# GpSimd leaves the experts' weights: ScalarE makes every hi part, VectorE every lo part

## The chip, the cores and the metric

One core of a Trainium2 chip runs the whole program. The metric is device time in microseconds; "before" is the median of three runs. The profile is one execution of the same program, and its times count from the first instruction.

## The reference

The program chains an attention with pooled queries, a layer of eight experts with top-1 routing, and a dense layer with a cosine gate. What matters here is the middle:

```python
x = attention output, 2304 tokens x 512
do_compute = (x @ w_skip) > 0
logits = xc @ w_gate;  e_idx = argmax(logits)          # eight experts
for e in range(E):
    h = np.maximum(xc[mask] @ w1[e], 0.0)              # 512 x 1024
    y[mask] = gate_w[mask, None] * (h @ w2[e])         # 1024 x 512
out[do_compute] = xc + y
```

All is float32. The kernel keeps that precision by splitting every operand of a product into a rounded hi part and the rest, the lo part, and adding three products (hi by hi, lo by hi, hi by lo).

## The kernel before

**Stages.** Attention runs until about 559 us of the profile, the experts from there to about 762 us, the last layer to the end. Only the experts' stage contains what is changed.

**Pieces of weights.** An expert's weights are eight pieces of 128 x 1024 float32 (512 KB): four of w1, four of w2. Eight experts give 64 pieces, numbered in `self.count` in the order in which `Experts.piece` is called. For each piece, SyncE's queue issues a load into one of six staging buffers (L699; the first six are loaded before the stage begins), one engine copies it to the hi part (L706 GpSimd or L708 ScalarE, a rounding copy), and one engine subtracts to make the lo part (L709, GpSimd or VectorE). hi and lo lie in `whl`, which has ten buffers: piece k + 10 can be made only when TensorE has done with piece k. A staging buffer is free for the next load when both parts are made.

**Which engine makes which part** stands in two lists by hand: 18 of the 64 hi parts (`HPOOL`) and 15 of the lo parts (`LPOOL`) are GpSimd's. A loop at the end that takes left-over blocks has lists of its own (`HREST`, `LREST`); for these inputs it runs no round, as the counts of 64 hi and 64 lo parts in the trace show.

**Blocks.** An expert's tokens go in blocks of 256, 128 or 64 rows; `GROUPS` says which expert by rank has which blocks, thirteen in all. Four experts have a single block of 64 rows, so a whole expert's weights are made for little TensorE work. A block is transposed (`transposed`, TensorE to PSUM, then ScalarE L686 makes hi and VectorE L687 lo), multiplied with w1 (`mm1`), its hidden rows are made (L746/L747 for 256 rows; L754, L755 and the transposes with L683/L684 for 64 rows), multiplied with w2 (`mm2`), and scaled by the gate (L798, L800). Tokens are fetched and results scattered by indirect transfers that GpSimd issues (L633, L801).

**Routing of the last batch** lies at the start of the stage: GpSimd adds the last logits (L336 to L343), VectorE runs a chain of small operations (L469 to L511), a small product of TensorE stands in that chain (L497 to L502), and GpSimd scatters the lists (L519). The second weights of the first expert (pieces 4 to 7) are asked for with `issue_after(self.placed.ins)`: what they issue on VectorE stands behind the end of that chain (L511); what they issue on other engines does not.

**Order.** A planner turns the program into one fixed queue per engine before the run: it goes through the program by priority, which is mostly program order, with its own idea of durations, and gives an engine the first instruction that it holds to be ready. On the chip every engine takes its queue in order, and waits at the head of it.

Of the kernel before, what the change touches and what calls it, by code (L numbers as in the profile page):

```python
# [8 lines left out]
F32 = mybir.dt.float32  # L9
# [9 lines left out]
NB, NH, NS, ND = 4, 8, 1152, 64     # batches, heads, keys, head width  # L19
NQ = NS // 2                        # pooled queries of a batch  # L20
NT = NB * NQ                        # tokens
DM, NE, FF, FF2 = 512, 8, 1024, 2048
CAP = NT                            # list rows an expert has: every token fits
NJ = 12                             # entries of the tables of pairs and of single blocks
LIST = NE * CAP + 128 * 28          # the rest of the list stays empty
TR = 4 * NJ + 1                      # where the ranks of experts start in the tables
BIG = 1 << 20                       # a row index that is out of bounds everywhere
# The blocks of rows that experts take: the one with the most tokens of all batches but the last, a first block of
# FIRST rows and then these; the others by their rank in how many tokens they have. A loop takes all that is left
# [4 lines left out]
NXT = 6                             # buffers for gathered tokens  # L34
QS = -0.0625                         # halves the sum of two queries, and scales scores by -1 / sqrt(ND)
OFFS = {'s0': 3, 's1': 2, 'r0': 2, 'r1': 2, 'n': 2, 'e0': 2, 'e1': 2, 't0': 1, 't1': 1, 's2': 2, 'r2': 2, 'e2': 1, 'h1': 1}
POOLP = ((5, 1), (6, 2), (7, 0))  # (chunk, piece) whose p parts GpSimd makes
STEPS = 'l1 r0 h0 e2 p4 s1 t2 s2 r2 l0 r1 h2 n x t1 t0 l2 e1 f s0 e0 p3 p2 a h1 p4'
NCH = 6
POPS = (0, 7, 8)               # chunks after which a step of the routing goes  # L40
# [6 lines left out]
LAG = 5                             # products that the second ones of the last layer run behind  # L47
ORDERS = ('1 1 1 1 r 1 w t g g g h', '2 2 2 2 2 x x g 1 1 1 1 1 h', '1 2 1 2 1 2 x 2 1 1 g 2 h', '1 x 1 1 1 g 2 2 2 1 h 2 2', '1 1 2 x 1 1 2 1 h 2 2 g 2', '1 1 1 2 x 2 1 2 2 1 h 2', 'x 1 g 1 1 1 2 1 h 2 2 2 2', '1 g 1 1 1 1 x 2 2 2 2 2 g h', '1 1 x 1 1 1 h 2 2 2 2 2', 'g 1 1 1 x 2 1 2 2 1 h 2 2 g', '1 1 x 1 1 2 2 1 2 h 2 2', '1 1 1 x 2 2 1 2 2 1 h 2', '1 1 1 2 1 2 1 2 h 2 2')
ORDER = "1 1 x 1 1 1 2 2 h 2 2 2 g"    # steps of a block that is left
HPOOL = (5, 7, 8, 15, 21, 29, 36, 37, 39, 42, 45, 47, 48, 52, 53, 54, 58, 62)  # L50
LPOOL = (6, 9, 11, 16, 21, 22, 23, 30, 38, 40, 45, 56, 57, 62, 63)
HREST, LREST = (1, 4, 6), (3,)


class Attention:
    def __init__(self, tc, ctx, stage, q, k, v, ident, pair_done, extra=lambda: None, last=lambda c: None, n_pairs=16):
# [5 lines left out]
        # the first to be free at the end come first, where the experts' first weights go  # L62
# [14 lines left out]
        # sums of the parts of a chunk's rows, and what is added to them  # L77
# [16 lines left out]
    def start(self):  # L94
        """load the first pair and make its operands: each head's q and k go to both halves of the partitions"""
        nc, s = self.nc, self.st.setdefault(0, {})
        raw = self.pb.tile([128, 9, 640], F32R, name="ptbigh").bitcast(F32).rearrange("p a b -> p (a b)")
        # the first activation loads its table, which need not wait for data
# [54 lines left out]
    def preps(self, i):  # L153
        """the steps that make pair i's operands, in order"""
# [55 lines left out]
    # chunk order within a pair, with the column it takes in its pT tile  # L210
# [4 lines left out]
    def scores(self, i, c, n):  # L215
        """a third of the scores of a chunk, times -1 / sqrt(ND)"""
        nc, s = self.nc, self.st[i]
        kind, j = self.CH[c]
        if kind == "X":
            qx, khl = s["qx"], s["khl"]  # L220
            prods = [(qx[:, 0, :], khl[:, 0, :]), (qx[:, 1, :], khl[:, 0, :]), (qx[:, 0, :], khl[:, 1, :])]
        else:
            h = 0 if kind == "A" else 1
            qa, k1 = s["qa"][h], s["k1"][h]
            prods = [(qa[:, t, 128 * j:128 * j + 128], k1) for t in range(2)]
        o = s["s", c, n] = self.pss.tile([128, 512], F32, name="s")
        for t, (w, m) in enumerate(prods):
            nc.tensor.matmul(o[:, 0:384], w, m[:, 384 * n:384 * n + 384], start=t == 0, stop=t == len(prods) - 1)  # L228
# [53 lines left out]
    # AV groups: head, pT tile, first column, columns, chunks whose sums they need  # L282
# [3 lines left out]
    def av_ops(self, i, key):  # L286
        """the steps of an AV group, in order, as callables"""
# [32 lines left out]
    def out_part(self, i, key):  # L320
        """token-major output of an AV group, and what it adds to the routing logits"""
# [5 lines left out]
        # the third has only 64 rows; what stands in the others goes nowhere  # L327
# [79 lines left out]
class Router:  # L407
    """top-1 routing: per expert a list in DRAM of (token, gate) pairs, in regions of CAP rows"""
# [9 lines left out]
    def start(self):  # L418
# [6 lines left out]
        # constants: e * CAP, 8 - e, valid rows, token numbers, counting matrices  # L425
# [14 lines left out]
        # tri[k, m] = 1 where k < m  # L440
# [11 lines left out]
        # per head: what sums the two halves of an output of attention, and gives its logits  # L452
# [6 lines left out]
    def route(self, b, L, ps, tag="tp"):  # L459
        """the lists' entries of a batch from its logits; a list of steps"""  # L460
# [4 lines left out]
    def choose(self, b, L, box):  # L465
# [15 lines left out]
        # the first expert that has the maximum  # L481
# [10 lines left out]
    def place(self, ps, tag, box):  # L492
        """place within the expert: tokens before it in its tile, in earlier tiles, in earlier batches"""
# [24 lines left out]
    def scatter(self, t, box):  # L518
# [3 lines left out]
        # the rows that different scatters write are different  # L522
# [4 lines left out]
    def counts(self, ps, tag):  # L527
        """how many tokens each expert has so far, and numbers in that order that are all different"""
# [6 lines left out]
    def ahead(self, ps, tag, tab):  # L535
        """the expert with the most tokens so far, whose first block is taken as it is now: in tab from TR + 2 NE on, its
        number, the first list row of its region, and the first one that is left"""
# [15 lines left out]
    def rank(self, ps, tag, tab):  # L553
        """the experts in the order of how many tokens they have, but the one whose first block has been taken as the
        last: in tab from TR on, their numbers, then the first list rows of their regions. In begin, the tokens of each
        that the blocks of its rank take"""
# [23 lines left out]
    def plan(self, ps, tag, tab):  # L580
        """the blocks of the other tokens, as pairs and at most one single block per expert. In tab, NJ
        each: experts and first list rows of the pairs, then those of the single blocks; last, the loop's end"""
# [11 lines left out]
        # blocks, pairs, single ones of each expert, and of one more that has no tokens and no end  # L594
# [33 lines left out]
def gathered(nc, pool, xg, lt, name, xt=None, n=NT, rows=128):  # L628
    """the tokens of a list; rows that no token fills keep what was there, and are dropped in the end"""
# [8 lines left out]
class Experts:  # L638
    def __init__(self, tc, ctx, stage, early, xts, w1, w2, ident, xg, x2, lst):
# [4 lines left out]
        # a pool has to wait for all that lay where it lies: the first weights have one of their own  # L644
# [19 lines left out]
    def transposed(self, srcs, nch, rows, relu=False):  # L664
        """hi and lo parts of the transposes of the column blocks of one or two sources of 128 rows, or of one of 64:
        then, lo stands beside hi"""
# [23 lines left out]
    def piece(self, w, e, c, n):  # L690
# [9 lines left out]
        hp, lp = (self.count in HPOOL, self.count in LPOOL) if self.laid_out else (n in HREST, n in LREST)  # L700
# [4 lines left out]
        if hp:  # L705
            nc.gpsimd.tensor_scalar(hi, raw, 1.0, 0.0, ALU.mult, ALU.add)  # L706
        else:
            nc.scalar.copy(hi, raw)  # L708
        (nc.gpsimd if lp else nc.vector).tensor_tensor(lo, raw, hi.bitcast(F32), ALU.subtract)  # L709
        return hi, lo  # L710

    def weights(self, group, k, c):
        """pieces up to c of an expert's first (k = 0) or second weights, which all its blocks use"""
        w = group["w"][k]
        while len(w) <= c:
            w.append(self.piece((self.w1, self.w2)[k], group["e"], len(w), 4 * k + len(w)))
        return w[c]

    def mm1(self, group, xT, rows):
        """steps: four products, and what leads to the hidden rows (one block) or their transposes (two)"""  # L720
# [4 lines left out]
        def product(c):  # L725
            hi, lo = self.weights(group, 0, c)
            if rows == 256:
                # the weights stay put, and both blocks pass them
# [36 lines left out]
    def products(self, o, xT, rows, c, hi, lo, first, last, b=0):  # L765
        """adds the products of a block's rows with a piece of weights: of 64 rows, hi and lo parts pass hi as one, and
        what they give is still to be added"""
# [13 lines left out]
    def mm2(self, group, hT, g, rows):  # L781
        """steps: four products, and the rows of the result"""
# [26 lines left out]
    def run(self, groups, first=None, route=None, plan=None):  # L809
        """groups: functions that give an expert and the first list row of its blocks, and the blocks' rows with where  # L810
        they start; first: the lists of the first block, if it is there before the others, which route (a list of
        steps) and plan then make"""
        self.laid_out = first is not None
# [61 lines left out]
def narrow(nc, pool, src, tag, g=None, n=512):  # L875
    """n columns of float64, which come as pairs of int32 words, as float32"""
# [5 lines left out]
    # sign and top exponent bit, the low 7 exponent bits, 23 bits of the mantissa  # L882
# [3 lines left out]
    # what is below float32's range (an exponent under 897, read as a float32 one: 2^-15) becomes zero  # L886
# [7 lines left out]
class Ffn:  # L894
    """out = (h cos h) w_out, h = x w_in"""
# [42 lines left out]
    def xT(self, x, tags):  # L938
        """hi and lo parts of a chunk's transpose, and the steps that make them"""
# [14 lines left out]
    def hidden(self, x, f, m):  # L954
        """what leads to hi and lo parts of -g / 2 = (sin^2(r / 2) - 1 / 2) h, r = h - 2 pi k: r, and a step for the
        rest"""
# [37 lines left out]
    def run(self):  # L994
# [3 lines left out]
        # two chunks of 384 tokens at a time  # L998
# [85 lines left out]
def build(tc, q, k, v, wg, ws, w1, w2, w_in64, w_out64, out):  # L1084
    nc = tc.nc
    w_in64, w_out64 = w_in64.bitcast(I32), w_out64.bitcast(I32)
    with ExitStack() as top:
# [9 lines left out]
        with ExitStack() as mid:  # L1097
# [9 lines left out]
            # staging buffers that attention loads into, and then the experts, whose first weights come before its end  # L1107
# [6 lines left out]
            def ranked(j):  # L1114
                """the expert of rank j: its number, its first list row"""
# [97 lines left out]
```

## Time and profile before

| | |
|---|---|
| runs | 1210.28, 1212.82, 1219.66 us; median 1212.82 |
| profiled execution | span 1214.5 us, the only time given of it |
| experts' stage in it | about 559 to 762 us |
| TensorE's mean granted clock | 0.978 of 2.4 GHz |
| hi parts of pieces | 46 by ScalarE, 18 by GpSimd |
| lo parts of pieces | 49 by VectorE, 15 by GpSimd |

In the rows below PE is TensorE's products, PEld its weight loads, DVE is VectorE, ACT ScalarE, POOL GpSimd. A line number is that of the kernel before. An arrow in brackets names what ended a wait.

### The profile page before, as it was taken

Reading aid. Unit: us, or ns where it says so; the run is one execution under the profiler, and the core shown is the slowest. Engines: PE = TensorE matmul, PEld = TensorE weight load, DVE = VectorE, ACT = ScalarE, POOL = GpSimd, SP = SyncE. Lnnn points to the kernel's source line nnn. Section 1 sums busy time; section 2 is a strip of 40 time slices with the busy share of each in tenths; the row PEclk is TensorE's granted clock in tenths of the full one; section 3 lists DMA queues with packets and bytes.
Section 4 is the critical chain, followed back from the end, with each engine's and each line's share of the span. In section 5 each row is a group of like instructions: output and inputs, shape, how many; then the busy total and the mean of one; then the engine's idle time right before and its main releaser. Section 6 shows DMA issues by size and latency. Waiting matters only on the chain. (4 is left out here: it accounts for less than half of the span.)

```text
span 1214.5 us, 20655 instructions
## 1 busy us (share of the span) xinstructions
PE 1124.1 (93%) x6722; PEld 1006.4 (83%) x6722; DVE 952.4 (78%) x1942; ACT 758.1 (62%) x1998; POOL 650.0 (54%) x861
## 2 busy tenths in 40 slices
PE   3999999999999999997989997688997999999998
PEld 3989899899898999897767874578886999889987
DVE  7889899999899999897788667498898755565554
ACT  3889898899888999795245312444544544454343
POOL 7587667766577666736656525265454423222331
PEclk9999999999999999998999998889999999999999
DMA  6575566456765675433568534632221200010001
GB/s 180 141 200 146 152 202 177 125 154 166 215 168 141 162 212 142 115 101 122 176 217 290 174 99 148 195 97 79 55 68 35 105 1 1 1 53 1 1 1 53
DMA packets 62639, 147.73 MB, mean 122 GB/s; under 512 B 17882, under 2 KB 17882, under 8 KB 62528
## 3 DMA queue, kind: packets, MB, share of 16 engines
q1 hardware_dynamic: 59840, 141.75, 40.4%
q0 software_dynamic: 2688, 4.62, 1.1%
q8 instruction: 55, 0.90, 0.3%
q14 instruction: 56, 0.46, 0.1%
HBM read 91.93 MB, written 21.69 MB: 94 GB/s over the span
## 5 line engine op out<-in xcount | busy, mean ns | idle before, releaser
L237 DVE TENSOR_REDUCE m<-s 128x1 f32<-128x384 f32 x432 | 236.7, 552 | 49.0 <-PE s L228 38.4
L246 ACT ACTIVATE p<-s,m 128x384 f32<-128x384 f32 x432 | 247.8, 583 | 22.4 <-DVE m L241 19.5
L228 PE MATMUL s<-k,qa 128*128 128x384 f32 x768 | 228.9, 382 | 32.1 <-ACT p L246 16.9
L264 PE MATMUL tp<-ident,p 128*128 128x128 f32 x1296 | 203.8, 277 | 4.6 <-DVE ptsml L280 2.3
L264 PEld LDWEIGHTS tp<-ident,p 128*128 128x128 f32 x1296 | 164.1, 143 | 17.8 <-issue 2.2
L228 PEld LDWEIGHTS s<-k,qa 128*128 128x128 f32 x768 | 120.4, 195 | 41.6 <-ACT p L246 26.0
L966 ACT ACTIVATE t<-hp,magic 128x384 f32<-128x384 f32 x96 | 55.6, 579 | 138.6 <-PE hp L963 137.1
L963 PE MATMUL hp<-fxh,wih 128*128 128x384 f32 x384 | 131.7, 344 | 8.5 <-ACT h L967 7.2
L968 POOL TENSOR_SCALAR t<-t 128x384 f32<-128x384 f32 x96 | 60.5, 631 | 135.5 <-ACT t L966 132.6
L963 PE MATMUL hp<-fxl,wih 128*128 128x384 f32 x384 | 130.3, 339 | 0.0
L963 PE MATMUL hp<-fxh,wil 128*128 128x384 f32 x384 | 130.2, 339 | 0.0
L992 PE MATMUL o<-woh,gh 128*128 128x512 f32 x288 | 115.7, 402 | 3.2 <-ACT woh L926 3.2
L992 PE MATMUL o<-wol,gh 128*128 128x512 f32 x288 | 115.5, 401 | 1.5 <-DVE wol L929 1.5
L992 PE MATMUL o<-woh,gl 128*128 128x512 f32 x288 | 115.0, 399 | 0.0
L280 DVE TENSOR_TENSOR ptbigl<-tp,ptbigh 128x384 fp32r<-128x384 f32 x208 | 112.3, 544 | 0.1
L978 POOL TENSOR_SCALAR gh<-h 128x384 fp32r<-128x384 f32 x96 | 70.4, 746 | 77.6 <-DVE h L976 69.2
L969 DVE TENSOR_TENSOR r<-t,h 128x384 f32<-128x384 f32 x96 | 67.4, 702 | 52.1 <-POOL t L968 51.6
L976 DVE SCALAR_TENSOR_TENSOR h<-r,h 128x384 f32<-128x384 f32 x96 | 56.4, 622 | 57.7 <-ACT r L975 57.7
L275 ACT CAST ptbigh<-tp 128x384 fp32r<-128x384 f32 x208 | 94.0, 490 | 11.2 <-PE tp L264 10.5
L280 DVE TENSOR_TENSOR ptsml<-tp,ptsmh 128x384 fp32r<-128x384 f32 x176 | 95.1, 545 | 0.7 <-ACT ptsmh L275 0.7
L275 ACT CAST ptsmh<-tp 128x384 fp32r<-128x384 f32 x176 | 81.4, 489 | 21.0 <-PE tp L264 15.4
L709 DVE TENSOR_TENSOR whl<-stage,whl 128x1024 fp32r<-128x1024 f32 x49 | 79.5, 1644 | 16.6 <-POOL whl L706 11.6
(239 smaller groups left out, 2906.2 us busy)
## 6 DMA issues: line engine op xcount, KB each, us to landing
stage<-w SPq DMA_DIRECT2D x64, 512.0 KB, 4.1
k<-stage SPq DMA_DIRECT2D x60, 288.0 KB, 5.4
qa<-stage SPq DMA_DIRECT2D x60, 256.0 KB, 5.1
stage<-v SPq DMA_DIRECT2D x16, 576.0 KB, 6.4
stage<-q SPq DMA_DIRECT2D x15, 576.0 KB, 4.7
stage<-k SPq DMA_DIRECT2D x15, 576.0 KB
wiw<-w_in SPq DMA_DIRECT2D x16, 512.0 KB, 4.5
wow<-w_out SPq DMA_DIRECT2D x16, 512.0 KB, 3.7
```

What stands on the lines that cost most here:

```text
L228: nc.tensor.matmul(o[:, 0:384], w, m[:, 384 * n:384 * n + 384], start=t == 0, stop=t == len(prods) - 1)
L237: self.last_max = nc.vector.tensor_reduce(s["m", c][:, n:n + 1], s["s", c, n][:, 0:384], AX.X, ALU.min)
L246: self.nc.scalar.activation(s["p", c][:, 384 * n:384 * n + 384], s["s", c, n][:, 0:384], AF.Exp, bias=s["m", c][:, 3:4], scale=-1.0, accum ...
L264: nc.tensor.transpose(tp[:, a, :], p[:, (3 * n + a) * 128:(3 * n + a + 1) * 128], self.ident)
L275: self.nc.scalar.copy(hi, tp)
L280: self.nc.vector.tensor_tensor(lo, tp, hi.bitcast(F32), ALU.subtract)
L709: (nc.gpsimd if lp else nc.vector).tensor_tensor(lo, raw, hi.bitcast(F32), ALU.subtract)
L963: nc.tensor.matmul(hp, w[:, d], a[:, d], start=d + k == 0, stop=d == 3 and k == 2)
L968: nc.gpsimd.tensor_scalar(t, t, -self.MAGIC, -self.C1, ALU.add, ALU.mult)
L969: nc.vector.tensor_tensor(r, t, h, ALU.add)
L978: nc.gpsimd.tensor_scalar(gh, h, 1.0, 0.0, ALU.mult, ALU.add)
L992: self.nc.tensor.matmul(o[t], a[:, s], w, start=f + k == 0, stop=f == 15 and k == 2)
```

## The change

In `piece` the choice of engine is gone: the hi part is always ScalarE's copy and the lo part always VectorE's subtraction. The lists `HPOOL`, `LPOOL`, `HREST`, `LREST`, the flag `laid_out` and the argument `n` that only fed them go with it. The rest of the diff removes comments.

```diff
-HPOOL = (5, 7, 8, 15, 21, 29, 36, 37, 39, 42, 45, 47, 48, 52, 53, 54, 58, 62)
-LPOOL = (6, 9, 11, 16, 21, 22, 23, 30, 38, 40, 45, 56, 57, 62, 63)
-HREST, LREST = (1, 4, 6), (3,)
...
-    def piece(self, w, e, c, n):
+    def piece(self, w, e, c):
...
-        hp, lp = (self.count in HPOOL, self.count in LPOOL) if self.laid_out else (n in HREST, n in LREST)
...
-        if hp:
-            nc.gpsimd.tensor_scalar(hi, raw, 1.0, 0.0, ALU.mult, ALU.add)
-        else:
-            nc.scalar.copy(hi, raw)
-        (nc.gpsimd if lp else nc.vector).tensor_tensor(lo, raw, hi.bitcast(F32), ALU.subtract)
+        nc.scalar.copy(hi, raw)
+        nc.vector.tensor_tensor(lo, raw, hi.bitcast(F32), ALU.subtract)
...
-            w.append(self.piece((self.w1, self.w2)[k], group["e"], len(w), 4 * k + len(w)))
+            w.append(self.piece((self.w1, self.w2)[k], group["e"], len(w)))
```

## Rows read from the trace of the kernel before

**Rows 1.** The page's first part: busy us, share of the span, instructions.
```profile
PE 1124.1 (93%) x6722; PEld 1006.4 (83%) x6722; DVE 952.4 (78%) x1942; ACT 758.1 (62%) x1998; POOL 650.0 (54%) x861
```

**Rows 2.** Busy time by stretch: us, each engine, granted clock, DMA share, GB/s.
```profile
555.00:762.00 207.00, 183.00 (x968) 142.33 (x966) 152.98 (x216) 70.17 (x96) 113.29 (x78) 0.95 0.52 179
...
560.00:580.00 20.00, 14.38 (x99) 13.74 (x100) 11.36 (x26) 3.51 (x7) 14.68 (x17) 0.83 0.44 147
...
600.00:680.00 80.00, 74.88 (x403) 57.01 (x403) 69.06 (x71) 38.97 (x51) 53.69 (x30) 0.98 0.72 252
...
620.00:640.00 20.00, 15.90 (x69) 11.11 (x67) 17.31 (x16) 8.70 (x10) 14.87 (x9) 0.91 0.72 234
...
680.00:700.00 20.00, 16.98 (x104) 14.98 (x103) 11.20 (x11) 4.15 (x6) 6.64 (x4) 0.91 0.37 124
...
740.00:760.00 20.00, 13.92 (x57) 8.32 (x56) 16.87 (x17) 4.40 (x6) 14.13 (x7) 0.88 0.33 107
```

**Rows 3.** TensorE's waits, 550 to 765 us: total us, times, longest.
```profile
PE ops L773 <- DVE hTh L684: 6.3, 3, 3.1
PE tp L680 <- DVE hs L755: 4.9, 5, 2.4
PE hps L734 <- DVE hTl L747: 3.0, 1, 3.0
PE rk L497 <- DVE oh L489: 2.4, 1, 2.4
...
PE ops L779 <- DVE whl L709: 0.3, 1, 0.3
```

**Rows 4.** Timeline of PE where the last layer begins.
```profile
768.87 0.90 PE L948 MATMUL o<-ident,fx 128*128 128x128 f32 x3 [7.97 <-DMA fx<-x]
```

**Rows 5.** Groups by line, 550 to 760 us: busy us, mean ns, idle before.
```profile
L709 DVE TENSOR_TENSOR whl<-stage,whl 128x1024 fp32r<-128x1024 f32 x49 | 79.5, 1644 | 16.6 <-POOL whl L706 11.6 <-ACT whl L708 5.0
L708 ACT CAST whl<-stage 128x1024 fp32r<-128x1024 f32 x46 | 47.6, 1052 | 40.8 <-DMA stage<-w 22.3 <-PE hps L773 9.9 <-issue 2.7
...
L709 POOL TENSOR_TENSOR whl<-stage,whl 128x1024 fp32r<-128x1024 f32 x15 | 40.4, 2702 | 9.6 <-ACT whl L708 9.3
...
L706 POOL TENSOR_SCALAR whl<-stage 128x1024 fp32r<-128x1024 f32 x18 | 20.6, 1153 | 25.2 <-PE hps L773 18.7 <-DMA stage<-w 6.3
```

**Rows 6.** The line of the lo parts: duration ns min/median/max, first and last start.
```profile
L709 DVE TENSOR_TENSOR whl<-stage,whl x49: 1206/1224/3427, 555.6 to 753.6; 128x1024 fp32r<-128x1024 f32 x49
```

**Rows 7.** Timeline of the stage's start, POOL, DVE and PE: start, us.
```profile
560.32 2.02 POOL L706 TENSOR_SCALAR whl<-stage 128x1024 fp32r<-128x1024 f32 x1
...
565.05 2.37 POOL L709 TENSOR_TENSOR whl<-stage,whl 128x1024 fp32r<-128x1024 f32 x1 [1.87 <-ACT whl L708]
...
565.11 2.34 DVE L477 TENSOR_SCALAR gate<-gate 128x5 f32<-128x5 f32 x1
...
565.02 0.38 PE L734 MATMUL hps<-xTl,whl 128*128 128x256 f32 x1 [1.65 <-DVE xTl L687]
```

**Rows 8.** Timeline around 622 us, POOL, DVE and PE.
```profile
620.73 2.41 POOL L709 TENSOR_TENSOR whl<-stage,whl 128x1024 fp32r<-128x1024 f32 x1
...
620.80 3.42 DVE L709 TENSOR_TENSOR whl<-stage,whl 128x1024 fp32r<-128x1024 f32 x1 [1.25 <-POOL whl L706]
...
625.54 0.80 PE L773 MATMUL ops<-whl,hTh 128*128 128x512 f32 x1 [3.06 <-DVE hTh L684]
```

**Rows 9.** Timeline around 683 us, DVE, POOL and PE.
```profile
679.70 4.82 DVE L709 TENSOR_TENSOR whl<-stage,whl 128x1024 fp32r<-128x1024 f32 x2
...
680.18 3.26 POOL L709 TENSOR_TENSOR whl<-stage,whl 128x1024 fp32r<-128x1024 f32 x1
...
686.62 0.54 PE L734 MATMUL hps<-xTh,whl 128*128 128x256 f32 x2 [3.02 <-DVE hTl L747]
```

**Rows 10.** Groups by line, 600 to 680 us.
```profile
L709 DVE TENSOR_TENSOR whl<-stage,whl 128x1024 fp32r<-128x1024 f32 x26 | 42.2, 1640 | 6.2 <-POOL whl L706 3.2 <-ACT whl L708 3.0
...
L709 POOL TENSOR_TENSOR whl<-stage,whl 128x1024 fp32r<-128x1024 f32 x9 | 22.9, 2548 | 4.5 <-ACT whl L708 4.4
```

More of the change, by code (lines that the diff above doesn't have):

```diff
@@ L809, in run @@
     def run(self, groups, first=None, route=None, plan=None):
-        self.laid_out = first is not None
         groups = [{"get": get, "base": base, "blocks": blocks, "w": ([], [])} for get, base, blocks in groups]
```

## The prediction

> **What bounds the kernel now.** I read the page's first part, then busy time by stretch, then what TensorE waits for. TensorE is busy 93% of the span [rows 1], so the question is only what it loses in the stage that is changed. That stage lasts 207 us, and no engine but TensorE is near full: 183.0 us TensorE, 153.0 VectorE, 113.3 GpSimd, 70.2 ScalarE; DMA is at 0.52 [rows 2]. TensorE hardly ever waits for a piece itself: 0.3 us once. It waits for VectorE's other work: the lo part of a 64-row block's hidden rows (6.3 us), its two halves' sum (4.9), the hidden rows of a 256-row block (3.0), the routing (2.4) [rows 3]. These operations stand behind lo parts of pieces in VectorE's queue. Each such wait is seen again in the granted clock: it is 0.83 in 560 to 580 us and 0.91, 0.91 and 0.88 in the stretches of the later waits [rows 2]. With levels of 1 and 0.5, that is TensorE work lost of 20 x 0.17 = 3.4 us, then 1.8, 1.8 and 2.4. At the stage's end TensorE waits 7.97 us for the last layer's tokens [rows 4]; nothing of the change lies there.
>
> So at most some 25 to 30 us of the stage can be won: waits of about 17 us [rows 3] and 9.4 us of clock.
>
> **Part 1: what each part costs on its engine.** A lo part takes VectorE 1.22 us at the median, but 1.644 at the mean and 3.43 at most [rows 5, 6]. The long ones lie where GpSimd runs a part of its own: at 620.80 VectorE's took 3.42 us, and GpSimd's had begun at 620.73 and taken 2.41; VectorE's ended 1.1 us after it, as if it had begun when GpSimd's ended [rows 8]. At 679.70 two took 4.82 us around one of GpSimd's [rows 9]. A small step of the routing chain, on 128 x 5 numbers, took 2.34 us from 565.11; GpSimd's lo part ran from 565.05 for 2.37 [rows 7]. So a part on GpSimd holds up VectorE, and what the lists were to save is largely paid back.
>
> The sum for VectorE: 15 lo parts more at 1.22 = +18.3 us. Relief: 49 x (1.644 - 1.224) = -20.6 us [rows 5, 6], and 2.2 us of the routing step. VectorE ends at 153.0 + 18.3 - 22.8 = 148.5 us: no more than before. In the dense stretch, 600 to 680 us, it is 9 x 1.22 = +11.0 against 26 x 0.416 = -10.8 [rows 10]. Bounds of the relief: all of it, or none if the length has another cause; I take all, since the three rows above fit to 0.2 us.
>
> ScalarE gets 18 hi parts at 1.05 = +18.9 us, and has 70.2 of 207 [rows 2, 5]: throughput covers it. GpSimd loses 40.4 + 20.6 = 61 us [rows 5]; it is then left with indirect transfers, which come no later. Loads: a staging buffer is free when both parts are made, 1.05 + 1.22 = 2.3 us of work on ScalarE and VectorE in place of 1.15 + 2.70 = 3.9 where GpSimd made both [rows 5], so SyncE's queue is not held longer on that account; DMA at 0.72 in the dense stretch has room [rows 2].
>
> **Part 2: what lies on the path,** from the profile's span of 1214.5 us, which is 1.7 above the median of the runs.
>
> *Start, 560 to 570 us.* GpSimd's lo part no longer stands before the routing step, which ends about 2.2 us sooner. On VectorE this piece goes behind the chain, by the order that the code writes for pieces 4 to 7. The 2.4 us wait for the routing falls by 2.2. GpSimd's hi part of 560.32 (2.02 us) stands before its last logits, on which the chain hangs, and the 1.65 us wait before may shrink with it [rows 7]. Against it, that hi part now can stand before the first tokens' hi part on ScalarE: 0 to 1.05. I take -2.2 + 0.5 = -1.7 (bounds -4.0 to +1.1). Of the clock's 3.4, half: -1.7 (0 to -3.4), since a shorter wait may still lower it.
>
> *622 us.* The lo part in the way falls from 3.42 to 1.22, and GpSimd's part of 620.73 becomes one more of 1.22 that may stand there too: -1.0 (-3.1 to +0.3) of a wait of 3.06. Clock: a third of 1.8, -0.6.
>
> *683 us.* Two lo parts fall from 4.82 to 2.44, one comes: -1.2 (-3.0 to 0) of 3.02. Clock -0.6.
>
> *740 to 760 us.* Four lo parts come to VectorE, 4.9 us, in the last 64-row blocks, against relief of about the same size; 0 (-2.5 to +2.5), and of 2.4 us of clock nothing.
>
> *ScalarE's queue.* GpSimd's hi parts stood waiting 25.2 us, 18.7 of it for TensorE to release a buffer and 6.3 for a load [rows 5]. These waits now stand at the head of ScalarE's queue, with evacuations of PSUM (L686, L683, L746) behind them, and TensorE and VectorE wait for those. Bounds: 0, if the planner puts them where ScalarE is idle anyway, to +8, a third. As ScalarE is idle two thirds of the time, +1.0.
>
> Sum: -1.7 - 1.7 - 1.0 - 0.6 - 1.2 - 0.6 + 0 + 1.0 = **-5.8 us**: 1208.7 by the profile, **1207** by the median of the runs.
>
> The Trainium skill, "Perfetto Trace Analysis", section "Optimizing Scalar/DVE Operations", says that where VectorE is saturated, giving work to ScalarE or even GpSimd may make sense, which speaks against this change, and in the same paragraph that GpSimd and VectorE share a read port, so that moving work between those two might not help. By the first sentence alone the lists are worth the 18.3 us that they spare VectorE, and the outcome is the rival "VectorE becomes the bound"; by the second it is the sum above. The rows of 620.80 and 565.11 bear out the second; no row shows VectorE full over a stretch.
>
> **The rivals.**
> *All of it comes back.* If each of the first three waits falls below what lowers the clock, waits and clock go together: -4.0 - 3.4 - 3.1 - 1.8 - 3.0 - 1.8 = -17, and with +1 for ScalarE -16: 1197. For: clock and waits lie together in every stretch of rows 2. Against: in two of the three places an added lo part may stand in the same spot.
> *VectorE becomes the bound (slower).* If the long lo parts don't shorten as said, the stretch from 600 to 680 us has 69.06 + 11.0 = 80.1 us of VectorE work in 80 [rows 2, 10]; its queue never empties, every evacuation in it comes later, and TensorE pays the 11.0, less some 3 won at the start: +8, 1221; with all 18.3 unpaid, 1231. It decides from the point where less than about half of the 10.8 comes back. Against: three rows that fit.
> *ScalarE's queue holds.* A hi part that waits for a buffer or a load stands before an evacuation several times: +8 in place of +1, which gives 1214, and with the first places won only by half 1217. For: ScalarE's own hi parts already wait 22.3 us for loads and 9.9 for buffers [rows 5]. Against: the planner hands out what it holds ready.
> *Nothing to be seen.* Relief and addition fall on the same places and the planner's new order wins as much as it loses: 1213.
>
> **How the numbers follow.** Forecast (1202 to 1212) 0.47, all back 0.17, VectorE the bound 0.13, ScalarE's queue 0.11, nothing 0.12. The range leaves out the better half of "all back" and the upper half of "VectorE": 1197 to 1225. One per cent, 12 us, is about what a measurement here can tell from no change (the three runs span 0.8%). Below 1200.7: "all back" and a little of the forecast's edge, 0.18. Above 1225: most of "VectorE" and an edge of "ScalarE's queue", 0.12. Within: 0.70.
>
> **What would show it.** Right: all 64 lo parts on VectorE near 1.22 us, mean under 1.3; VectorE's busy time in the stage at or under 153; the routing step short, and TensorE's wait for the routing under 1 us; shorter waits for L684 and L747; a clock above 0.83 in the first stretch. Wrong: lo parts still long without GpSimd; a stretch in which VectorE has no idle time; ScalarE's hi parts waiting with L683, L686 or L746 late behind them; or the planner's new order moving TensorE's work in a way that no step here names.

## The result and the profile after

The changed kernel takes 1199.57 us (median of four runs, 1194.12 to 1202.32) against 1211.63 of the kernel before on the same chip (median of four). The ratio on record is 0.9865, with a 95% interval of 0.9831 to 0.9899; it is not the ratio of these two medians, which is 0.990. By it the change is worth 16 us; the medians lie 12.1 us apart, and the spans of the two profiled executions 13.9. 5.8 were forecast. All us given for runs below are worked out from the ratio on record and the median of the kernel before. The profiled execution has a span of 1200.6 us; its run is listed with 1202.32, so 1.7 us lie around the span.

The page's first part, which answers to [rows 1]. GpSimd loses 66 us, ScalarE gains 18, and VectorE, which has 15 more lo parts to make, is busy 6 us less.
```profile
PE 1119.4 (93%) x6722; PEld 1002.4 (83%) x6722; DVE 946.3 (79%) x1957; ACT 775.9 (65%) x2016; POOL 584.4 (49%) x828
```

Busy time by stretch (us; each engine; granted clock; DMA share; GB/s): first the stage, then its start and the stretches that answer to those around 620, 683 and 750 us of [rows 2].
```profile
554.00:747.00 193.00, 180.68 (x971) 140.80 (x969) 146.75 (x232) 88.42 (x115) 48.47 (x46) 0.96 0.55 192
559.00:579.00 20.00, 17.75 (x121) 16.79 (x121) 12.21 (x34) 7.49 (x12) 10.56 (x14) 0.83 0.44 151
617.00:637.00 20.00, 19.94 (x95) 14.05 (x95) 19.20 (x22) 11.69 (x14) 6.64 (x4) 1.00 0.80 275
672.00:692.00 20.00, 19.90 (x138) 17.59 (x138) 10.88 (x14) 6.49 (x10) 1.89 (x2) 1.00 0.46 161
725.00:745.00 20.00, 14.35 (x57) 9.17 (x56) 15.75 (x19) 5.47 (x7) 3.29 (x2) 0.83 0.31 101
```
TensorE's products fill the second and third of these short stretches (19.9 of 20 us, clock 1.00, where before they had 15.9 and 17.0 at 0.91). The last stretch is no better than before.

The line of the lo parts (min/median/max ns), which answers to [rows 6]:
```profile
L702 DVE TENSOR_TENSOR whl<-stage,whl x64: 1206/1215/1483, 555.0 to 740.5; 128x1024 fp32r<-128x1024 f32 x64
```
The groups of both parts in the stage, which answer to [rows 5]:
```profile
L702 DVE TENSOR_TENSOR whl<-stage,whl 128x1024 fp32r<-128x1024 f32 x64 | 76.6, 1221 | 11.1 <-ACT whl L701 10.9
L701 ACT CAST whl<-stage 128x1024 fp32r<-128x1024 f32 x64 | 66.2, 1054 | 55.5 <-DMA stage<-w 39.8 <-PE hps L772 5.8 <-SPq L1175 4.9
```
TensorE's waits in the stage, which answer to [rows 3]; the wait for the last layer's tokens is left out:
```profile
PE ops L766 <- DVE hTh L681: 2.2, 1, 2.2
PE tp L677 <- DVE hs L748: 2.0, 2, 1.5
PE hps L766 <- DVE xTh L684: 1.8, 1, 1.8
PE hps L765 <- DVE whl L702: 1.5, 1, 1.5
```
Without GpSimd's parts no lo part takes longer than 1.48 us, where the longest was 3.43. Sixty-four of them cost VectorE 76.6 us, less than the 49 before. The waits for the 64-row hidden rows and the halves' sums fell from 11.2 to 4.2 us; those for the routing and for the 256-row hidden rows are gone. The one for the first tokens of the second expert has grown from 0.33 to 1.8, and one for a lo part is new (1.5). VectorE's own waits for hi parts fell from 16.6 us [rows 5] to 10.9.

**Where the time went.** Both kernels do the same products, so TensorE's progress can be laid side by side: us from the stage's first transposition until so many thousand columns had passed TensorE, worked out from the start times of all its products (a transposition of 64 columns and less counted as 64). Each column is one profiled execution of a run named in the experiments below; after_again is the changed kernel a second time.
```
columns  before   after  after_again  read_dummies  write_dummies  lo_only  hi_only  tail_lo
   20k     17.73   14.40        11.78         12.68          11.79    14.41    11.79    14.11
   40k     26.88   23.54        20.93         22.35          20.94    23.57    20.96    23.28
   60k     36.89   34.99        32.91         36.67          32.32    33.60    38.62    34.71
  100k     57.65   55.73        53.65         57.40          53.06    54.35    59.32    55.45
  140k     83.76   76.29        74.26         78.75          73.59    75.24    79.85    76.02
  200k    115.67  109.29       106.82        113.53         106.11   109.60   111.95   110.72
  240k    139.22  128.42       125.61        136.34         125.16   128.83   130.73   129.52
  300k    167.85  156.44       153.64        164.36         153.18   157.50   158.75   157.54
  320k    183.75  166.29       163.48        175.00         163.03   172.38   168.60   167.38
  340k    199.78  185.38       182.34        194.06         182.31   192.76   182.13   180.73
  380k    234.55  219.43       217.47        229.02         217.39   228.07   217.39   215.15
```
After minus before: -3.3 at the start, +1.4 between 40 and 60 thousand, -5.5 between 100 and 140 (the wait at 622 us), +1.1 from there to 200, -4.4 between 200 and 240 (683 us), -0.6 to 300, -3.0 between 300 and 340 and -0.7 after that: -15.1 us. Outside the stage the two profiles differ by about 1 us (attention 0.6 sooner; last layer 1.2 longer).

The two columns of the changed kernel show how far one execution can be trusted. Between 40 and 340 thousand columns none of their steps differs by more than 0.6 us, but in the first 20 thousand they differ by 2.6. TensorE's waits there are the same four in both (0.8, 0.8, 0.6 and 0.5 us); the granted clock is not. It is 0.83 in after (559.00:579.00 above), as in the kernel before, and 1.00 in after_again (same columns as above):
```profile
550.00:570.00 20.00, 17.73 (x131) 16.41 (x131) 14.68 (x48) 7.88 (x13) 10.34 (x14) 1.00 0.45 147
```
So the step at the start is -3.3 us in one execution and -6.0 in another of the same kernel, and differences of up to 3 us between columns that arise in their first 20 thousand say nothing about a kernel. The steps at 622 and 683 us come out in both (-5.5 and -5.5, -4.4 and -4.8).

The timeline of VectorE at three places. First the routing step and VectorE's lo parts before the hidden rows, which answer to [rows 7] and [rows 8]; then the lo parts that answer to [rows 9].
```profile
563.49 0.17 DVE L474 TENSOR_SCALAR gate<-gate 128x5 f32<-128x5 f32 x1
...
616.52 1.21 DVE L702 TENSOR_TENSOR whl<-stage,whl 128x1024 fp32r<-128x1024 f32 x1
618.10 0.69 DVE L681 SCALAR_TENSOR_TENSOR hTh<-tp,hTh 128x512 fp32r<-128x512 f32 x1 [0.37 <-ACT hTh L680]
...
669.76 4.62 DVE L702 TENSOR_TENSOR whl<-stage,whl 128x1024 fp32r<-128x1024 f32 x4
674.60 1.29 DVE L740 SCALAR_TENSOR_TENSOR hTl<-hps,hTh 128x512 fp32r<-128x512 f32 x2 [0.21 <-ACT hTh L739]
```
The routing step takes 0.17 us in place of 2.34. At 674 us four lo parts have gone by in less than the 4.82 that two took, and VectorE is early: it waits 0.21 us for ScalarE's hidden rows, whereas before TensorE waited 3.02 for VectorE's. At 618 it is the same (0.37).

### The profile page after: what moved, and what is told of

Same layout as the page of the kernel before. It is cut to its first block, busy times and chain, and to the rows that moved or that the text cites. A ratio compares the mean times of both kernels' runs of the same rounds, so it can differ in the third digit from the quotient of the medians.

```text
span 1200.6 us, 20635 instructions
## 1 busy us (share of the span) xinstructions
PE 1119.4 (93%) x6722; PEld 1002.4 (83%) x6722; DVE 946.3 (79%) x1957; ACT 775.9 (65%) x2016; POOL 584.4 (49%) x828
## 5 line engine op out<-in xcount | busy, mean ns | idle before, releaser
L701 ACT CAST whl<-stage 128x1024 fp32r<-128x1024 f32 x64 | 66.2, 1054 | 55.5 <-DMA stage<-w 39.8
```

## The experiments

Each ratio is against runs of the kernel before on the same chip. The yardstick is the changed kernel once more, on one chip; runs on other chips are compared with it by their ratios:

> The changed kernel once more, as the yardstick of the runs beside it: 14 to 18 us under the kernel before by every theory.

Measured: 0.9864 (0.9839 to 0.9889), -16.4 us.

**Reading put back without anyone waiting for it.** For the places of the two old lists:
```diff
         nc.vector.tensor_tensor(lo, raw, hi.bitcast(F32), ALU.subtract)
+        n = self.count - 1
+        if n in HPOOL:
+            nc.gpsimd.tensor_scalar(self.dum, hi.bitcast(F32), 1.0, 0.0, ALU.mult, ALU.add)
+        if n in LPOOL:
+            nc.gpsimd.tensor_tensor(self.dum, hi.bitcast(F32), hi.bitcast(F32), ALU.subtract)
```


> The changed kernel, and GpSimd makes, for the same 33 parts as before, a result that nobody reads, from the piece's finished hi part. Theory 1 (a GpSimd part that reads SBUF holds up VectorE's two-input operations): VectorE's lo parts are long again, mean about 1.5 us or more, and most of the gain goes: 0 to 6 us under the kernel before. Theory 2 (GpSimd was late as a producer: others waited for its parts in its queue): nobody waits for these, so 12 to 17 us under. Theory 3 (the planner's new order of the queues is what helps): the orders of the other engines stay nearly those of the changed kernel, so 12 to 17 us under.

Measured: 0.9964 (0.9946 to 0.9983), -4.4 us. Twelve of the 16 us are gone.

**The same occupation of GpSimd, nearly without reading:**
```diff
...
+        for _ in range((n in HPOOL) + 2 * (n in LPOOL)):
+            nc.gpsimd.tensor_scalar(self.dum[:, 0:1], hi[:, 0:1].bitcast(F32), 1.0, 0.0, ALU.mult, ALU.add)
+            nc.gpsimd.memset(self.dum.bitcast(F32), 0.0)
```


> As the kernel with the results that nobody reads, but GpSimd fills a scratch tile (one fill in place of a hi part, two in place of a lo part) after reading one column of the finished hi part: as busy, with nearly no reading. Theory 1: VectorE's lo parts stay near 1.22 us and 12 to 17 us under the kernel before remain. Theory 2 in the form that GpSimd's queue delays its indirect transfers: 0 to 8 us under. Theory 3: 12 to 17 us under.

Measured: 0.9864 (0.9839 to 0.9888), as the changed kernel. The groups of lo parts and of GpSimd's idle results, with reading:
```profile
L705 DVE TENSOR_TENSOR whl<-stage,whl 128x1024 fp32r<-128x1024 f32 x64 | 88.0, 1398 | 9.2 <-ACT whl L704 9.2
...
L710 POOL TENSOR_TENSOR dum<-whl 128x1024 fp32r<-128x1024 f32 x15 | 35.7, 2381 | 6.3 <-issue 3.0 <-ACT whl L704 2.4
L708 POOL TENSOR_SCALAR dum<-whl 128x1024 fp32r<-128x1024 f32 x18 | 27.4, 1522 | 36.5 <-ACT whl L704 35.9
```
and with filling:
```profile
L705 DVE TENSOR_TENSOR whl<-stage,whl 128x1024 fp32r<-128x1024 f32 x64 | 76.6, 1221 | 11.2 <-ACT whl L704 11.2
...
L709 POOL MEMSET dum<- 128x1024 f32 x48 | 45.9, 957 | 2.6
...
L708 POOL TENSOR_SCALAR dum<-whl 128x1 fp32r<-128x1 f32 x48 | 23.4, 487 | 30.0 <-ACT whl L704 27.3
```
GpSimd is busy some 63 to 69 us with its idle work in both. Only when it reads do the lo parts stretch (88.0 against 76.6 us), and only then is the time lost. Theory 3 is out for this pair: in both traces TensorE's 6722, VectorE's 1957 and ScalarE's 2016 instructions stand in the same order as in the changed kernel, and no engine waits for an idle result. So theory 1 holds as a cause, and neither a busy GpSimd nor its queue costs anything here. The Trainium skill, "SBUF — State Buffer", section "Who interferes with whom", says that a VectorE instruction with two SBUF inputs contends with a GpSimd instruction that reads SBUF and not with one that only writes it; 1398 against 1221 ns agree.

**One kind of part alone.** In the kernel before, `LPOOL = ()` (lo_only), or `HPOOL = ()` (hi_only).

> The kernel before with only the 15 lo parts taken from GpSimd; the 18 hi parts stay with it. Theory 1: the lo parts are 40.4 of the 61 us that GpSimd read for, so about two thirds of the gain, 8 to 13 us under the kernel before, and lo parts of 1.25 to 1.4 us mean. Theory 2: VectorE's waits for parts were all for GpSimd's hi parts (11.6 us), so little of the gain comes, 0 to 6 us under. Theory 3: not foretold.

> The kernel before with only the 18 hi parts taken from GpSimd; the 15 lo parts stay with it. Theory 1 (a GpSimd part that reads holds up VectorE): 20.6 of 61 us go, so about a third of the gain, 3 to 7 us under the kernel before, and VectorE's lo parts keep a mean over 1.45 us. Theory 2 (GpSimd late as a producer of hi parts): most of the gain, 9 to 16 us under. Theory 3 (the planner's order): not foretold.

Measured: lo_only 0.9967 (0.9946 to 0.9987), -4.0 us; hi_only 0.9836 (0.9806 to 0.9866), -19.9 us. Theory 1 missed in both: the shares don't follow the us for which GpSimd reads, and the parts don't add. Theory 2 was right for lo_only (0 to 6 us) and said too little for hi_only (9 to 16). In lo_only the lo parts are nearly clean, and the time is lost all the same; in hi_only GpSimd reads for 41.5 us still, and nothing is lost. The group of lo parts in lo_only:
```profile
L709 DVE TENSOR_TENSOR whl<-stage,whl 128x1024 fp32r<-128x1024 f32 x64 | 81.3, 1296 | 17.8 <-ACT whl L708 9.3 <-POOL whl L706 8.4
```
One place near the end of its stage, in the timelines of VectorE and of SyncE's queue (SPq):
```profile
703.70 3.06 DVE L709 TENSOR_TENSOR whl<-stage,whl 128x1024 fp32r<-128x1024 f32 x1 [0.93 <-POOL whl L706]
...
706.79 0.33 SPq L699 DMA_DIRECT2D stage<-w  x1
...
718.86 2.05 DVE L709 TENSOR_TENSOR whl<-stage,whl 128x1024 fp32r<-128x1024 f32 x1 [5.71 <-POOL whl L706]
```
The same place in the kernel before (GpSimd, VectorE, SyncE's queue, VectorE), then the load in the changed kernel:
```profile
718.29 3.09 POOL L706 TENSOR_SCALAR whl<-stage 128x1024 fp32r<-128x1024 f32 x3
...
719.39 3.07 DVE L709 TENSOR_TENSOR whl<-stage,whl 128x1024 fp32r<-128x1024 f32 x1 [0.92 <-POOL whl L706]
...
722.49 0.33 SPq L699 DMA_DIRECT2D stage<-w  x1
...
735.30 2.05 DVE L709 TENSOR_TENSOR whl<-stage,whl 128x1024 fp32r<-128x1024 f32 x1 [6.47 <-POOL whl L706]
```
```profile
706.69 0.33 SPq L696 DMA_DIRECT2D stage<-w  x1
```
In lo_only GpSimd begins the hi part at 702.60, behind a scatter that it issues at 701.56. VectorE's subtraction for it then runs beside GpSimd's next hi part and takes 3.06 us, and the load that waits for its staging buffer is issued when it ends: 151.4 us after the stage's first transposition in lo_only, against 146.6 in the changed kernel. The hi part for which VectorE then waits 5.71 us had itself waited 3.08 for its load, so the end of this long wait hangs on the load. (Before, the profile names a product of TensorE, which frees a buffer of `whl`, as what the hi part of 735.30 waited for last.) TensorE needs 14.9 us from 300 to 320 thousand columns in lo_only and 15.9 before, against 9.9 in the changed kernel: one piece that is made late here, and the load that is late with it, go with a loss of some 5 us, while the lo parts are clean on the mean. This is read from the traces; no run takes this piece alone.

The groups of lo parts in hi_only:
```profile
L709 DVE TENSOR_TENSOR whl<-stage,whl 128x1024 fp32r<-128x1024 f32 x49 | 62.4, 1293 | 7.9 <-ACT whl L708 7.9
L709 POOL TENSOR_TENSOR whl<-stage,whl 128x1024 fp32r<-128x1024 f32 x15 | 41.5, 2776 | 29.6 <-ACT whl L708 29.5
```
With hi parts on GpSimd, VectorE waits 8.4 us for them, 5.71 at one place. Without them 11 of GpSimd's 15 lo parts still run beside one of VectorE's, but GpSimd's are stretched as well, up to 4.66 us, and VectorE's 49 have an excess of 3.5 us in all, against 20.6 before. Both theories are half right: a hi part on GpSimd is one that VectorE waits for, and its end also sets off a VectorE subtraction just when GpSimd begins its next part, as at 620.73 and 620.80 [rows 8]. In the trace before, four of VectorE's subtractions begin 0.06 to 0.11 us after a part of GpSimd's, and they take 2.01 to 3.42 us.

**Reading only, one kind of place alone.** From the kernel with reading, `LPOOL = ()` (read_hi) or `HPOOL = ()` (read_lo).

> The changed kernel, and GpSimd makes a result that nobody reads at the 18 places of its hi parts only. If hi parts on GpSimd cost because they read while VectorE subtracts: most of the 12 us that all such results cost come here, 6 to 12 us over the changed kernel. If they cost because VectorE waited for them: 0 to 4 us over it.

> The same at the 15 places of GpSimd's lo parts only. If what they hold up is what cost: 6 to 12 us over the changed kernel, since VectorE has its own 64 lo parts to make besides. If only both together cost: 0 to 4 us over it.

Measured: read_hi 0.9899 (0.9865 to 0.9934), read_lo 0.9886 (0.9842 to 0.9931): by these ratios about 4 and 3 us over the changed kernel, with intervals that reach to it, where both together cost 12. So reading at one kind of place costs little, and at both more than the sum by these figures; the difference, some 5 us, is not clear of the noise of the three runs.

**Which hi parts.** lo_only without its last five hi parts (52, 53, 54, 58, 62), and the changed kernel with only these five on GpSimd:

> The kernel before without any lo part on GpSimd and without its last five hi parts: 13 hi parts stay with it. If the last five made the run with 18 slow: 8 to 14 us under the kernel before. If the other 13 did: 3 to 7 us under.

> The changed kernel, but GpSimd makes five hi parts near the stage's end (52, 53, 54, 58, 62), all lo parts VectorE's. If GpSimd's hi parts are what made that stretch 35 us in place of 29 in the run without GpSimd's lo parts: 4 to 8 us over the changed kernel, with VectorE waiting for GpSimd's hi part. If it was the planner's order of that run: within 2 us of the changed kernel.

Measured: hi_not_tail 0.9920 (0.9892 to 0.9948), -9.7 us, so that of the 12.5 us by which lo_only is behind the changed kernel, the last five cost 5.7 and the other 13 cost 6.8; tail_hi 0.9887 (0.9862 to 0.9912), 2.8 us over the changed kernel, less than foretold and not clear of the noise. In the profiles TensorE's step from 300 to 320 thousand columns is 13.3 us in hi_not_tail and 11.1 in tail_hi, against 14.9 in lo_only and 9.9 in the changed kernel: most of the loss at the stage's end is there without the last five. So hi parts cost before the end too, and the last five cost little by themselves.

**One pair, one part.** The changed kernel with hi part 15 and lo part 16 on GpSimd (spot_both), or hi part 15 alone (spot_hi).

> The changed kernel, but GpSimd makes one hi part (15) and the next piece's lo part (16), the pair that collided at 620 us before. If that pair alone cost the 6.4 us of that stretch: 3 to 7 us over the changed kernel. If it needs GpSimd's queue as it was filled before: within 2 us of it.

> The changed kernel, but GpSimd makes one hi part (15). If the late hi part was most of the cost at 620 us before: 2 to 5 us over the changed kernel. If the collision of the two lo parts was: within 1 us of it.

Measured: 0.9870 (0.9838 to 0.9902) and 0.9842 (0.9810 to 0.9873), neither distinct from the changed kernel. In the profile of spot_both TensorE's time from 100 to 120 thousand columns is 12.1 us against 9.7 with neither or the hi part alone, and 16.1 before. The pair meets as it did before (GpSimd, then VectorE):
```profile
605.36 2.39 POOL L709 TENSOR_TENSOR whl<-stage,whl 128x1024 fp32r<-128x1024 f32 x1
...
605.41 3.42 DVE L709 TENSOR_TENSOR whl<-stage,whl 128x1024 fp32r<-128x1024 f32 x1 [0.23 <-POOL whl L706]
```
VectorE's subtraction takes 3.42 us, as at 620.80 [rows 8], but TensorE then waits 0.95 us for the hidden rows and not 3.06. So the collision alone makes part of the wait at 622 us: 2.4 of the 6.4 us of that step. Before, GpSimd's hi part 15 stood behind a fetch that had waited 6.26 us for its list; that this makes the rest is not shown by a run of its own.

**The start alone.** The kernel before without its GpSimd parts among pieces 5 to 9 (`HPOOL` from 15, `LPOOL` from 11).

> The kernel before with only pieces 5 to 9 taken from GpSimd, at the stage's start. The step of the prediction for the start said -3.4 us, and the two traces show -3.3 there up to 580 us: 2 to 5 us under the kernel before if steps add up; 0 if the later stretches take it back.

Measured: 0.9980 (0.9961 to 0.9999), -2.4 us (-0.1 to -4.7), where the two terms for the start came to -3.4.

**lo parts on GpSimd once the hi parts are gone.** The changed kernel with `LPOOL = (56, 57, 62, 63)` (tail_lo), and hi_only with `LPOOL` from 16 on (lo_from_16).

> The changed kernel, but GpSimd makes four lo parts near the stage's end (56, 57, 62, 63), all hi parts ScalarE's. Theory 1 in the form that a GpSimd part costs only where it coincides with VectorE's two-input work: at the end VectorE is what TensorE waits for, and sparing it 4 x 1.22 us gives 3 to 6 us under the changed kernel, as the run without GpSimd's hi parts had it there. In the form that every GpSimd part costs: 1 to 4 us over the changed kernel.

> The run without GpSimd's hi parts, less its first three lo parts (6, 9, 11), which stood before a wait of 5.7 us at 590 us. If that wait was theirs: 3 to 6 us under that run, so about 23 to 26 us under the kernel before. If another piece would make the same wait: within 2 us of that run.

Measured: tail_lo 0.9816 (0.9788 to 0.9844), 1187.24 us, the fastest, 5.8 us under the changed kernel's yardstick; lo_from_16 0.9823 (0.9780 to 0.9866), within 2 us of hi_only, though its interval of 5 us to either side leaves open what was asked. In its profile TensorE's wait at that place is 2.3 us in place of 5.7. In the table tail_lo passes from 320 to 340 thousand columns in 13.4 us against 19.1 for the changed kernel. Its timeline there, GpSimd, then VectorE:
```profile
715.32 5.17 POOL L709 TENSOR_TENSOR whl<-stage,whl 128x1024 fp32r<-128x1024 f32 x2 [6.14 <-ACT whl L708]
...
723.64 6.36 POOL L709 TENSOR_TENSOR whl<-stage,whl 128x1024 fp32r<-128x1024 f32 x2 [2.05 <-ACT whl L708]
...
720.40 0.69 DVE L684 SCALAR_TENSOR_TENSOR hTh<-tp,hTh 128x512 fp32r<-128x512 f32 x1 [0.31 <-ACT hTh L683]
```
and the same place of the changed kernel, VectorE, then TensorE:
```profile
738.62 1.21 DVE L702 TENSOR_TENSOR whl<-stage,whl 128x1024 fp32r<-128x1024 f32 x1
739.86 0.69 DVE L681 SCALAR_TENSOR_TENSOR hTh<-tp,hTh 128x512 fp32r<-128x512 f32 x1
...
740.61 0.80 PE L766 MATMUL ops<-whl,hTh 128*128 128x512 f32 x1 [2.18 <-DVE hTh L681]
```
At the end VectorE has no gap, and TensorE waits for hidden rows behind a lo part. There four lo parts on GpSimd are a gain. Most of what VectorE does beside them reads PSUM (L684, L754, L755, L798, L800), and none of it is longer than elsewhere; the one lo part of VectorE that falls inside one of GpSimd's takes 1.21 us, and GpSimd's is stretched to 3.98. That PSUM is the reason is not shown by a run of its own.

**The same idea in the last layer.** The changed kernel with all hi parts of w_out on ScalarE (last_hi: `WOH = tuple(range(16))`), and also all lo parts of w_in and w_out on VectorE (last_all: `WIL = tuple(range(16))`, `WOL = ()`).

> The changed kernel, and in the last layer ScalarE makes also the 13 hi parts of w_out that GpSimd makes (0.63 us each). If theory 1 is the general cause, VectorE gets up to 13 x 0.6 us back in the stretch from 790 to 910 us where it is about 90% busy: 2 to 8 us under the changed kernel. If TensorE is what bounds that stretch: within 2 us of it.

> As the one before, and VectorE makes also the 8 lo parts of w_in and the 2 of w_out that GpSimd makes (about 1.3 and 0.7 us there, 0.65 on VectorE): relief about as much as the addition, so within 3 us of the kernel before it in this list by theory 1; 4 to 7 us slower than it if VectorE is at its limit there and gets no relief.

Measured: 0.9884 (0.9856 to 0.9912) and 0.9862 (0.9830 to 0.9893): no gain over 0.9864, against theory 1's hope. In the profiles the time from the last layer's first transposition to the end is 449.4 and 445.3 us, against 446.9 for the changed kernel.

## Why the prediction was wrong

*The cost of each part.* Right. Lo parts came to 1.22 us, as taken; VectorE's busy time was to be 148.5 us in 207, and is 146.75 in a stage that is 14 us shorter. The relief of 20.6 us came in full.

*The start.* The total of -1.7 - 1.7 lies near the -3.3 of the profile and the -2.4 of start_only, but partly by luck. In the profile the waits gave back the -3.3, 2.4 of it the wait for the routing, and the clock nothing (0.83 as before); in after_again the clock stayed at its upper level and the step was -6.0. "Half" of the clock's 3.4 is neither of the two.

*622 us and 683 us.* Here it failed, in the terms for these two places: "GpSimd's part of 620.73 becomes one more of 1.22 that may stand there too: -1.0", "two lo parts fall from 4.82 to 2.44, one comes: -1.2", with a third of the clock's loss each: -1.6 and -1.8 us in all. Measured: -5.5 (of which 1.1 went again before 200 thousand columns) and -4.4. The waits vanished whole and the clock stayed at its upper level, because the added lo part does not stand before the hidden rows: VectorE reached them early. Working with one part less or more at the spot where the wait was seen left out that the subtractions before it had come late too, by being held up (3.18 us at 672.83) and by waiting for GpSimd's hi parts (1.25 us at 620.80, 1.94 at 677.96; 11.6 in the stage). That second cost was in [rows 5] and never entered the sum. hi_only shows how much hangs on it: without GpSimd's hi parts, and with its lo parts left, the kernel is 19.9 us faster.

*740 to 760 us.* Forecast 0; in the profile -3.0 between 300 and 340 thousand columns, made of -6.1 in the first half and +3.1 in the second. The first goes with the late load of 722.49 shown with lo_only, as far as traces can tell: the prediction compared the work that frees a staging buffer, 2.3 us against 3.9, found that "SyncE's queue is not held longer on that account", and so put loads at nothing. The second is VectorE's added work, the four lo parts there: tail_lo, with these four on GpSimd, is another 5.8 us faster. The clock is no better, as said.

*ScalarE's queue.* +1.0 forecast, +1.4 in the profile, and at one place. ScalarE waits at the head of its queue for a load, and the tokens' evacuation stands behind (ScalarE, then TensorE):
```profile
589.50 1.04 ACT L701 CAST whl<-stage 128x1024 fp32r<-128x1024 f32 x1 [9.38 <-DMA stage<-w]
590.45 0.85 ACT L683 CAST xTh<-tp 128x256 fp32r<-128x256 f32 x2
...
591.33 0.51 PE L766 MATMUL hps<-whl,xTh 128*128 128x512 f32 x1 [1.77 <-DVE xTh L684]
```

*The rivals.* The total is that of "All of it comes back", 1197 against 1199.57 measured, which was given 0.17. At 622 and 683 us its account holds (-4.9 and -4.8 against -5.5 and -4.4); elsewhere the agreement is luck: it had -7.4 at the start, where the two executions show -3.3 and -6.0, and nothing at the end, where they show -3.0 and -3.2. The slower one, VectorE as the bound, is ruled out for the dense stretch (17.3 of 20 us busy before, 19.2 after, and TensorE full), but is true of the stage's end, where VectorE's work does bound TensorE and tail_lo gains by it.

What stays open: how much of a hi part's cost is the waiting and how much the collisions. The parts do not add: hi parts cost 12.5 us without lo parts on GpSimd and 19.9 with them, and reading costs about 3 and 4 us at one kind of place and 12 at both. At the one load followed above, the hold-up is 1.8 us (3.06 against 1.22) of the 4.8 by which the load is late. The kernels with idle results keep the order of the changed kernel's queues; those in which many parts change engine (lo_only, hi_only, tail_lo) get orders of their own from the planner, and no run here holds these fixed.

## What to carry to other kernels

Before GpSimd is given elementwise work to spare VectorE, compare the mean of VectorE's two-input operations with their median: here the mean was a third higher, and the sparing was paid back. A mean near the median is no all-clear: in lo_only it was 6% above, and 12.5 us were lost, some 5 of them at one load. In this kernel the part that starts a chain (the hi part) did better on ScalarE, and the part at the chain's end was worth giving to GpSimd where VectorE was what TensorE waited for. And when a delay is taken out of a queue, price the whole wait downstream of it with its clock, not only the operation that stood in front.

## What was not expected of the hardware

GpSimd's fills of 128x1024 (957 ns each, 48 of them) left VectorE's subtractions at 1221 ns, while GpSimd operations that read stretched them to 1398 on the mean. A routing step on 128 x 5 numbers took 2.34 us beside a GpSimd subtraction and 0.17 without it, so a small operation can be held up too. Either side of a meeting can be the one that is stretched: GpSimd's subtraction took 3.98 us beside a VectorE one of 1.21 in tail_lo, VectorE's 3.42 beside one of 2.41 before. And the same kernel, with the same waits, had a granted clock of 0.83 over 20 us in one execution and 1.00 in another.
